# The second pair of heads turned by transposing transfers instead of by TensorE

## The chip, the cores and the metric

One core of one Trainium2 chip runs one program. Its engines are TensorE (PE: products; PEld: the loading of their stationary operand), VectorE (DVE), ScalarE (ACT), GpSimd (POOL) and SyncE (SP, here a queue that issues transfers; ScalarE issues some on a queue of its own). The metric is the time of one execution in microseconds (us). Of the kernel before there are three timed runs and one profiled execution.

## The reference, cut to what matters

Attention in which a query sees only the keys of its own cluster, then a two-layer block with a squared ReLU:

```python
B, H, S, D = 4, 8, 768, 64          # 16 clusters per head
q_assign = argmax(einsum('bhsd,hcd->bhsc', q_n, c_n))   # q_n, k_n, c_n: normalized
k_assign = argmax(einsum('bhsd,hcd->bhsc', k_n, c_n))
scores = q @ k.T / sqrt(D), and -1e9 where q_assign != k_assign
x = softmax(scores) @ v             # (B*S, H*D) = 3072 x 512
out = relu(x @ w_in) ** 2 @ w_out   # w_in 512 x 2048, w_out 2048 x 512
```

## The kernel before, in words

The attention part handles the heads in 16 pairs (four batches, four pairs each); the loop over `p` counts them from 0, and the text calls them the first, second, third and fourth pair. The second layer block follows and is not touched.

For each pair the queries and keys (128 x 768 words each) must be turned, so that the head's 64 columns lie on partitions: `qkT`, 12 blocks of 128. There are three ways in the kernel. `turn_first` turns the first pair by products with the identity, three blocks at a time, and copies them out of PSUM. `turn` (lines 289 to 303) does so for the second pair in three parts of eight products, which stand between the first pair's scores. From the third pair on, `split_words` (lines 307 to 321) lets ScalarE split each 32-bit word into its halves (two copies for the queries, two for the keys), stores them to DRAM (`words`), and `turn_words` (line 327) brings them back in one transposing transfer of 16-bit words.

A pair's steps on TensorE are then: `logits` (line 335), the products of all rows with the centroids; from them VectorE finds each row's cluster (`turn_logits`, `number`, lines 340 to 380), and the cluster numbers, called marks, go out (`far`) and come back (`rows`) by small transfers on SyncE. Nine tiles follow, counted from 0: six of 512 query columns and three that hold the last 256 twice. Each tile is a mask product of marks (line 456) and a score product (line 447) added in one PSUM bank; ScalarE takes the exponential (line 463) into `ex`, VectorE adds them up (line 466). Then come the products with V (line 481), the sums (line 500) and their reciprocals, which go to DRAM (`far_r`) and come back spread over partitions (`rb`). The banks of the scores (`ps_sc`) number three, and the logits and the sums of a pair take one of them in turn: tile n can begin when the exponential of tile n - 3 is done. The first pair's marks are not numbers but a one-hot tile `oh`, turned by TensorE (`turn_onehot`).

The order on every engine is the order of the code: the attention part is written as a schedule by hand. So an instruction that waits holds what stands behind it on its engine, and a transfer that waits holds the rest of its queue. The weights come in by `load_ahead` (line 128), one block in some pairs, three blocks at the start, all on SyncE.

A flag decides at the end whether a second, general program must run: `seen` holds the reciprocals of all sums, and `check_sums` counts those within bounds.

## Time and profile before

| | |
|---|---|
| timed runs | 863.5, 864.5, 865.63 us (median 864.5) |
| profiled execution | 863.94 us |
| its span | 862.0 us |
| PE busy | 852.3 us (99%) |
| DVE, ACT, POOL busy | 741.0 (86%), 452.3 (52%), 242.2 us (28%) |

The span runs from the first to the last instruction of the profile; the execution's own time is 1.94 us longer, and lies 0.56 us under the median of the timed runs. Times in the timeline are counted from the span's start.

### The profile page before, as it was taken

To read this page: it belongs to the slowest core of one execution; us is meant where nothing else is said; L and a number is where in the kernel's file an instruction comes from. 1 tells how busy PE (TensorE), PEld (TensorE's weight loads), DVE (VectorE), ACT (ScalarE), POOL (GpSimd) and SP (SyncE) were. 2 spreads that over 40 slices of the span, in tenths; PEclk is the share of its full clock that TensorE was granted. 3 is DMA by queue.
4 is the path that set the end of the run, shared out by engine and by line. 5 is a ranking of instruction groups with operands and counts; after the bars stand their busy time and mean duration, and the time that the engine had idled before them with its cause. 6 is when DMAs were issued, how large, how long until landed. Compare 5 with 4: busy or idle time off the path is not lost.

```text
span 862.0 us, 15526 instructions
## 1 busy us (share of the span) xinstructions
PE 852.3 (99%) x5883; PEld 648.9 (75%) x5883; DVE 741.0 (86%) x1189; ACT 452.3 (52%) x697; POOL 242.2 (28%) x202
## 2 busy tenths in 40 slices
PE   9999999999999999999999999999999999999997
PEld 5454444444444455557899999999999999999997
DVE  6798888888888899999779988789888898887786
ACT  5877766777775557752212692222269322693120
POOL 0000000000000046762466737130223902237000
PEclk9999999999999999999999999999999999999999
DMA  7787798677666217729895554459447895433542
GB/s 258 162 194 201 216 268 197 183 198 196 177 176 178 64 61 249 241 85 336 329 336 195 206 186 152 179 162 337 149 183 230 288 379 191 183 140 137 214 153 71
DMA packets 149443, 173.30 MB, mean 201 GB/s; under 512 B 57226, under 2 KB 126962, under 8 KB 146034
## 3 DMA queue, kind: packets, MB, share of 16 engines
q1 hardware_dynamic: 132802, 151.89, 55.8%
q10 hardware_dynamic: 16560, 20.35, 7.3%
q8 instruction: 48, 0.79, 0.4%
q14 instruction: 33, 0.27, 0.1%
HBM read 110.93 MB, written 50.27 MB: 187 GB/s over the span
## 4 chain that ended last, share of the span: by engine, by line
PE 88%; DVE 6%; DMA 2%; issue 1%; ACT 1%; POOL 1%; SPq 0%; DVEq 0%; POOLq 0%
PE bank L1365 23%; PE bank L1098 15%; PE sc L447 14%; PE av_a L481 10%; PE bank L1262 6%; PE av_b L481 5%; PE more L1098 5%; PE sc L456 4%; PE bank L811 3%; PE sc L335 1%; PE sc L500 1%; DMA wt<-w_far 1%; DVE g L1177 1%; DVE w_raw L155 1%; DVE g L767 1%
## 5 line engine op out<-in xcount | busy, mean ns | idle before, releaser
L463 ACT ACTIVATE ex<-sc 128x1024 f32<-128x1024 f32 x144 | 144.4, 1026 | 38.0 <-PE sc L447 31.9
L447 PE MATMUL sc<-qkT 64*128 64x512 f32 (+1 forms) x768 | 151.0, 484 | 0.0
L167 POOL TENSOR_TENSOR w_in<-w_in,w_raw 128x512 int32<-128x512 int32 x16 | 21.4, 1338 | 294.4 <-DVE w_in L159 278.2
L1083 POOL TENSOR_TENSOR g<-g,home 128x768 f32<-128x768 f32 x30 | 55.7, 1876 | 152.4 <-DVE home L1177 102.2
L447 PEld LDWEIGHTS sc<-qkT 64*128 64x128 f32 x768 | 67.1, 188 | 41.0 <-issue 29.8
L481 PE MATMUL av_a<-ex,v_raw 128*64 128x512 f32 x384 | 85.9, 596 | 0.0
L466 DVE TENSOR_TENSOR total<-total,ex 128x1024 f32<-128x1024 f32 x64 | 78.7, 1229 | 6.5
L1613 ACT COPY spare<-bank 128x128 f32<-128x128 f32 x35 | 9.2, 263 | 136.5 <-issue 84.8
L1365 PE MATMUL bank<-wt,l 128*128 128x128 f32 x544 | 72.0, 275 | 0.4 <-DVE l L557 0.4
L1365 PE MATMUL bank<-wt,home 128*128 128x128 f32 x552 | 70.5, 275 | 0.0
L1365 PEld LDWEIGHTS bank<-wt,l 128*128 128x128 f32 x544 | 66.2, 192 | 0.6 <-issue 0.5
L1365 PEld LDWEIGHTS bank<-wt,home 128*128 128x128 f32 x552 | 66.0, 192 | 0.0
L1177 DVE TENSOR_TENSOR g<-bank,g 128x384 f32<-128x384 f32 (+2 forms) x108 | 53.7, 506 | 13.0 <-PE bank L1098 8.4
L481 PEld LDWEIGHTS av_a<-ex,v_raw 128*64 128x64 f32 x384 | 26.2, 137 | 51.0 <-issue 50.3
L1067 ACT COPY home<-bank 128x384 f32<-128x384 f32 x66 | 30.9, 480 | 56.4 <-PE bank L1098 55.7
L456 PE MATMUL sc<-rows 64*128 64x512 bf16 (+1 forms) x360 | 60.5, 323 | 0.0
L787 ACT ACTIVATE g<-g 128x768 f32<-128x768 f32 (+1 forms) x77 | 55.7, 723 | 2.4
L786 ACT ACTIVATE g<-g 128x768 f32<-128x768 f32 (+1 forms) x77 | 54.8, 711 | 2.3 <-DVE g L1177 1.2
L481 PE MATMUL av_b<-ex,v_raw 128*64 128x256 f32 x384 | 44.2, 379 | 0.0
L456 PEld LDWEIGHTS <-rows 64*128 64x128 bf16 x360 | 18.5, 94 | 33.0 <-issue 29.2
L481 PEld LDWEIGHTS av_b<-ex,v_raw 128*64 128x64 f32 x384 | 27.6, 137 | 20.7 <-issue 5.7
L1365 PE MATMUL bank<-wt,g 128*128 128x128 f32 x304 | 38.8, 275 | 0.0
(296 smaller groups left out, 1852.5 us busy)
## 6 DMA issues: line engine op xcount, KB each, us to landing
wt<-right_far SPq DMA_DIRECT2D x11, 1792.0 KB
wt<-w_far SPq DMA_DIRECT2D x20, 896.0 KB
words<-flat SPq DMA_DIRECT2D x26, 384.0 KB
w_raw<-in_moe_w_in_dram SPq DMA_DIRECT2D x16, 512.0 KB
w_raw<-in_moe_w_out_dram SPq DMA_DIRECT2D x16, 512.0 KB
wt<-right_far SPq DMA_DIRECT2D x7, 1024.0 KB
v_raw<-in_v_dram SPq DMA_DIRECT2D x16, 384.0 KB
rb<-far_r SPq DMA_DIRECT2D x30, 192.0 KB
```

The lines of the kernel that those rows point to most:

```text
L447: nc.tensor.matmul(sc[i][:, e, cols], lhsT=qkT[pair][rows, NCH + c], rhs=qkT[pair][rows, n.start // P : n.stop // P], start=first, stop=no ...
L456: nc.tensor.matmul(sc[i][:, e, cols], lhsT=ohT[pair][rows, 1, c * P : (c + 1) * P], rhs=ohT[pair][rows, 0, columns(i)], start=first, stop= ...
L463: nc.scalar.activation(out=ex[i], in_=sc.pop(i), func=ACT.Exp, scale=SCALE)
L466: eng.tensor_tensor(out=out, in0=a, in1=b, op=ALU.add)
L481: nc.tensor.matmul(bank[D * e : D * (e + 1), 0 : n.stop - n.start], lhsT=raw_v[pair][:, e, c], rhs=ex[i][:, e, cols], start=c == 0, stop=c ...
L786: nc.scalar.activation(out=to, in_=to, func=ACT.Relu)
L787: nc.scalar.square(to, to)
L1083: nc.gpsimd.tensor_tensor(out=of_four(to, s)[:, :, half], in0=of_four(base, s)[:, :, half], in1=beside[s].rearrange("p u m n -> p (u m) n" ...
L1098: nc.tensor.matmul(bank[:, QT * u : QT * (u + 1)], lhsT=lefts[j, s](u)[i], rhs=operand[i], start=begins and u == 0, stop=True, skip_group_ ...
L1177: nc.vector.tensor_tensor(out=out, in0=one, in1=two, op=ALU.add)
L1262: nc.tensor.matmul(bank, lhsT=left[j][:, f], rhs=right(j)[:, f], start=begins and f == 0, stop=True, skip_group_check=True,)
L1365: nc.tensor.matmul(bank, lhsT=left[:, f], rhs=rhs[:, f], start=(f == 0), stop=(f == F4 - 1))
```

## The change

The second pair is turned like the later ones: ScalarE splits it at the very start (into two tiles of `ex` instead of `flat`), issues the two stores on its own queue, and SyncE brings it back in two transposing transfers of half the size. `turn` is gone. The first pair's one-hot marks are set directly where a logit equals the row's maximum, without choosing among equal maxima; `count_marks` counts them, and another count than one per row makes the flag call the general program. The copy of the first pair's last three blocks is shared by ScalarE and VectorE (`by_two`). In the first pair the scores of all three first tiles come ahead of the masks, and the second pair's logits stand behind the eighth tile, in the bank `M`. The second pair scores two tiles ahead of its masks. Moved on SyncE's and ScalarE's queues: the second pair's rows go ahead of the third pair's turning, as before; V of the second pair is loaded behind that; of three weight blocks one is loaded in the first pair and two in the second; the fourth pair's keys are split in the second pair, behind the third tile, and the fifth pair's loads follow there.

```diff
-    seen = const.tile([P, NG * NBL], F32, name="seen")
+    seen = const.tile([P, NG * NBL + 1], F32, name="seen")
-    def turn(pair, part, bank):
...
-                nc.tensor.matmul(
-                    bank[D * e : D * (e + 1), P * i : P * (i + 1)],
-                    lhsT=raw[pair][which][:, e, c], rhs=ident, start=True, stop=True,
-                )
-        nc.scalar.copy(
-            out=qkT[pair][:, 4 * part : 4 * part + 4].rearrange("p c n -> p (c n)"), in_=bank
-        )
...
     def split_words(pair, which, queue=nc.sync):
-        flat = loads.tile([P, NCH, 2, 2 * D], U16, name="flat", tag="qk")
+        if pair == 1:
+            spare = expp.tile([P, 2, 512], F32, name="ex").bitcast(U16)
+            flat = spare.rearrange("p a n -> p (a n)")[:, 0 : 4 * S // 2].rearrange(
+                "p (c two d) -> p c two d", c=NCH, two=2
+            )
+        else:
+            flat = loads.tile([P, NCH, 2, 2 * D], U16, name="flat", tag="qk")
...
     def turn_words(pair):
-        nc.sync.dma_start(
-            qkT[pair].rearrange("p c n -> p (c n)").bitcast(U16),
-            words.pop(pair).rearrange("c p two d -> (c p two) d"), transpose=True,
-        )
+        far = words.pop(pair)
+        for i in range(0, 2 * NCH, NCH if pair == 1 else 2 * NCH):
+            c = slice(i, i + (NCH if pair == 1 else 2 * NCH))
+            nc.sync.dma_start(
+                qkT[pair][:, c].rearrange("p c n -> p (c n)").bitcast(U16),
+                far[c].rearrange("c p two d -> (c p two) d"), transpose=True,
+            )
...
     def number(pair):
         nc.vector.reduce_max(out=mx, in_=src, axis=AX.X)
+        if pair == 0:
+            nc.vector.tensor_tensor(
+                out=oh.rearrange("p b e c -> p (b e) c")[:, :, 0:C], in0=src, in1=over_c(mx),
+                op=ALU.is_ge,
+            )
+            return
...
+    def count_marks():
+        marked = small.tile([P, 1], F32, name="marked")
+        nc.vector.reduce_sum(
+            out=marked, in_=oh.rearrange("p b e c -> p (b e) c")[:, :, 0:C], axis=AX.XY
+        )
+        nc.vector.tensor_scalar(
+            out=seen[:, NG * NBL :], in0=marked, scalar1=2.0 * NBL, scalar2=0.5,
+            op0=ALU.is_equal, op1=ALU.mult,
+        )
...
-    turn_first(1, 1, halves[1], nc.vector.tensor_copy)
+    turn_first(1, 1, halves[1], by_two)
     logits(0, begin("ls"))
-    for i in ("oh", 0, 1):
+    for i in range(2):
         begin(i)
     turn_logits(0)
     number(0)
+    for i in range(2):
+        split_words(1, i, nc.scalar)
...
         if p == 0:
+            turn_words(1)
             load_qk(3)
-            load_ahead(0)
+            load_ahead(-2)
...
-        load_v(p + 1)
         if p:
+            load_v(p + 1)
             load_ahead(p - 1)
         if p == 0:
             for i in range(2):
-                turn(1, i, (V, M)[i])
                 score(p, i, 0, True)
             turn_onehot()
+            count_marks()
             for t in rows_of:
                 nc.vector.memset(t, 0.0)
-            turn(1, 2, V)
+            begin(2)
+            score(p, 2, 0, True)
             for i in range(NB):
-                if i == 2:
-                    begin(i)
-                    score(p, i, 0, True)
                 mask(p, i, 0, False)
                 exponential(i)
+        elif p == 1:
+            for i in range(2):
+                begin(i)
+                score(p, i, 0, True)
+            for i in range(2):
+                mask(p, i, 0, False)
+                exponential(i)
+            tile_of(p, 2)
+            split_words(3, 1)
+            turn_words(3)
+            load_qk(4, (nc.scalar, nc.scalar))
...
         for i in range(NCH, NCH + NB):
             tile_of(p, i)
+            if p == 0 and i == NCH + 1:
+                sc["ls"] = M.rearrange("p (a n) -> p a n", a=1)
+                logits(1, sc["ls"])
+                turn_logits(1)
+                number(1)
+                turn_words(2)
+                load_v(1)
+                add(nc.vector, first, first, ex[NCH - 1])
...
         if p == 0:
             split_words(3, 0)
-        split_words(p + 3, 1)
-        load_qk(p + 4, (nc.scalar, nc.scalar))
+        else:
+            split_words(p + 3, 1)
+            load_qk(p + 4, (nc.scalar, nc.scalar))
```

What moves on three engines, as the two programs list their instructions. First TensorE, from the first pair's logits on, before (a score tile is two products of line 447):

```order
L335 MATMUL sc<-qkT,cnT 32x384 x4
L295 MATMUL av_a<-ident,q_raw 64x128 x8
L447 MATMUL sc<-qkT 128x512 x2
L295 MATMUL av_b<-ident,q_raw 64x128 x4
L295 MATMUL av_b<-ident,k_raw 64x128 x4
L447 MATMUL sc<-qkT 128x512 x2
```

and with the change, where the second pair's logits (`av_b` is the bank `M`) stand far behind, between the first pair's last two tiles:

```order
L328 MATMUL sc<-qkT,cnT 32x384 x4
L450 MATMUL sc<-qkT 128x512 x4
```

```order
L450 MATMUL sc<-qkT 128x256 x2
L328 MATMUL av_b<-qkT,cnT 32x384 x4
L459 LDWEIGHTS ex
L459 MATMUL sc<-ex 128x256
```

The turning products of the second pair are gone, eight more of them behind the turning of the one-hot marks too, and the scores follow the logits directly.

Second ScalarE, from the last exponentials of the first pair to the fourth one of the second pair, before:

```order
L463 ACTIVATE ex<-sc 128x1024 x3
L315 COPY flat<-q_raw 128x12x64 x2
L315 COPY flat<-k_raw 128x12x64 x2
L95 DMA q_raw<-in_q_dram 128x2x384
L95 DMA k_raw<-in_k_dram 128x2x384
L139 ACTIVATE w_in<-w_raw 128x512
L145 ACTIVATE w_raw<-w_raw 128x512
L490 COPY xT<-av_a 128x512
L490 COPY xT<-av_b 128x256
L463 ACTIVATE ex<-sc 128x1024 x6
```

and with the change:

```order
L466 ACTIVATE ex<-sc 128x1024 x3
L305 COPY flat<-q_raw 128x12x64 x2
L139 ACTIVATE w_in<-w_raw 128x512
L145 ACTIVATE w_raw<-w_raw 128x512
L493 COPY xT<-av_a 128x512
L493 COPY xT<-av_b 128x256
L466 ACTIVATE ex<-sc 128x1024 x3
L305 COPY flat<-k_raw 128x12x64 x2
L95 DMA q_raw<-in_q_dram 128x2x384
L95 DMA k_raw<-in_k_dram 128x2x384
L466 ACTIVATE ex<-sc 128x1024 x3
```

The split of the fourth pair's keys and the fifth pair's loads have moved from behind the first pair's exponentials to between the second pair's third and fourth.

Third SyncE, from the third pair's turning to the third pair's rows (`rows_167`), before:

```order
L327 DMA_TRANSPOSE qkT<-words 128x3072
L316 DMA words<-flat 128x6x256 x2
L515 DMA far_r<-seen 128x12
L327 DMA_TRANSPOSE qkT<-words 128x3072
L522 DMA rb<-far_r 64x768 x2
L105 DMA v_raw<-in_v_dram 128x2x384
L383 DMA far<-marks_t 128x3x32
L386 DMA rows_167<-far 3x4x384 x2
```

and with the change:

```order
L320 DMA_TRANSPOSE qkT<-words 128x3072
L105 DMA v_raw<-in_v_dram 128x2x384
L306 DMA words<-flat 128x6x256
L518 DMA far_r<-seen 128x12
L525 DMA rb<-far_r 64x768 x2
L105 DMA v_raw<-in_v_dram 128x2x384
L128 DMA w_raw<-in_moe_w_in_dram 128x1024 x2
L306 DMA words<-flat 128x6x256
L320 DMA_TRANSPOSE qkT<-words 128x3072
L376 DMA far<-marks_t 128x3x32
L379 DMA rows_167<-far 3x4x384 x2
```

The second store of the fourth pair and its turning now stand behind the spreading, a load of V and two weight loads, directly ahead of the third pair's marks and rows.

## Rows read from the trace of the kernel before

**Rows 1.** The page's first part: busy us (share of the span) xinstructions.

```profile
PE 852.3 (99%) x5883; PEld 648.9 (75%) x5883; DVE 741.0 (86%) x1189; ACT 452.3 (52%) x697; POOL 242.2 (28%) x202
```

**Rows 2.** Timeline of PE, first pair: start us, us, engine line op out<-in xcount.

```profile
9.32 1.09 PE L295 MATMUL av_a<-ident,q_raw 128*64 128x128 f32 x16
10.35 1.13 PE L447 MATMUL sc<-qkT 64*128 64x512 f32 x4
...
15.29 0.61 PE L456 MATMUL sc<-ex 64*128 64x512 bf16 x4
...
16.97 0.85 PE L335 MATMUL sc<-qkT,cnT 128*32 128x384 f32 x8
17.89 0.39 PE L456 MATMUL sc<-ex 64*128 64x512 bf16 x2
```

**Rows 3.** Timeline of PE, first pair's products with V to third pair's masks.

```profile
24.48 5.37 PE L481 MATMUL av_a<-ex,v_raw 128*64 128x512 f32 x24
...
33.15 0.39 PE L456 MATMUL sc<-rows 64*128 64x512 bf16 x2
...
39.54 0.38 PE L456 MATMUL sc<-rows 64*128 64x512 bf16 x2
...
53.29 0.79 PE L456 MATMUL sc<-rows 64*128 64x512 bf16 x2
```

**Rows 4.** Timeline of ACT, first pair; in brackets idle time before and what ended it.

```profile
6.87 0.48 ACT L285 COPY qkT<-sc 128x384 f32<-128x384 f32 x1 [0.18 <-PE sc L280]
...
14.04 0.87 ACT L410 ACTIVATE ex<-sc 128x384 bf16<-128x384 bf16 x2 [0.90 <-PE sc L402]
...
15.89 2.86 ACT L463 ACTIVATE ex<-sc 128x1024 f32<-128x1024 f32 x3
...
22.24 1.55 ACT L315 COPY flat<-q_raw 128x768 uint16<-128x768 uint16 x2
...
26.36 1.94 ACT L463 ACTIVATE ex<-sc 128x1024 f32<-128x1024 f32 x2 [0.46 <-ACT flat L315]
```

**Rows 5.** Timeline of DVE: the first pair's copy, the third pair's marks.

```profile
7.95 0.56 DVE L285 COPY qkT<-sc 128x384 f32<-128x384 f32 x1 [0.52 <-PE sc L280]
...
38.58 0.58 DVE L346 STREAM_TRANSPOSE lt<-sc 128x384 f32<-128x384 f32 x1 [0.77 <-PE sc L335]
...
42.50 0.28 DVE L379 STREAM_TRANSPOSE marks_t<-marks 128x96 bf16<-128x96 bf16 x1
```

**Rows 6.** Timeline of SyncE's queue: start and length of each issue.

```profile
23.24 0.38 SPq L383 DMA_DIRECT2D far<-marks_t  x1
26.61 1.68 SPq L386 DMA_DIRECT2D rows<-far  x2
28.76 6.77 SPq L327 DMA_TRANSPOSE qkT<-words  x1
...
40.01 3.70 SPq L327 DMA_TRANSPOSE qkT<-words  x1
...
50.48 1.52 SPq L386 DMA_DIRECT2D rows<-far  x2
52.05 1.00 SPq L316 DMA_DIRECT2D words<-flat  x2
...
56.32 2.75 SPq L327 DMA_TRANSPOSE qkT<-words  x1
...
64.79 1.52 SPq L386 DMA_DIRECT2D rows<-far  x2
66.42 0.38 SPq L105 DMA_DIRECT2D v_raw<-in_v_dram  x1
...
75.64 3.21 SPq L327 DMA_TRANSPOSE qkT<-words  x1
```

**Rows 7.** Stretches of time: busy us per engine, PEclk, DMA share, GB/s.

```profile
9.00:11.00 2.00, 2.00 (x22) 1.15 (x20) 1.50 (x3) 0.54 (x1) 0.00 (x0) 1.00 1.07 386
...
58.00:59.00 1.00, 1.00 (x9) 0.64 (x7) 0.97 (x5) 0.95 (x2) 0.00 (x0) 1.00 1.21 276
```

More of the change, by code (lines that the diff above doesn't have):

```diff
@@ L287, in turn_first @@
             raw.pop(0)
-    def turn(pair, part, bank):
-        if part == 0:
-            qkT[pair] = qktp.tile([P, 2 * NCH, P], F32, name="qkT")
-        for i in range(4):
-            which, c = divmod(4 * part + i, NCH)
-            for e in range(2):
-                nc.tensor.matmul(
-                    bank[D * e : D * (e + 1), P * i : P * (i + 1)],
-                    lhsT=raw[pair][which][:, e, c], rhs=ident, start=True, stop=True,
-                )
-        nc.scalar.copy(
-            out=qkT[pair][:, 4 * part : 4 * part + 4].rearrange("p c n -> p (c n)"), in_=bank
-        )
-        if part == 2:
-            raw.pop(pair)
     words = {}
@@ L362, in number @@
         nc.vector.reduce_max(out=mx, in_=best, axis=AX.X)
-        if pair == 0:
-            nc.vector.tensor_tensor(
-                out=oh.rearrange("p b e c -> p (b e) c")[:, :, 0:C], in0=best, in1=over_c(mx),
-                op=ALU.is_equal,
-            )
-            return
         squared = small.tile([P, n], F32, name="squared")
@@ L395, in turn_onehot @@
         )
-        for half, bank in enumerate((sc.pop("oh")[:, 0], M)):
+        for half, bank in enumerate((V, M)):
             n = NBL // 2
@@ L607, in load_ahead, with by_two @@
             loaded += 1
+    def by_two(out, in_):
+        nc.scalar.copy(out=out[:, 0:QT], in_=in_[:, 0:QT])
+        nc.vector.tensor_copy(out=out[:, QT:], in_=in_[:, QT:])
+    QT = TB // 2
     centroids_norm()
@@ L639 @@
                 early_x_sums()
-            turn_words(p + 2)
+            if p > 1:
+                turn_words(p + 2)
             spread(p - 1)
@@ L671 @@
             tile_of(p, NB)
-        if p < 2:
             logits(p + 1, begin("ls"))
@@ L679 @@
                 tile_of(p, i)
-            add(nc.vector, first, first, ex[i])
+            if p or i + 1 < NCH:
+                add(nc.vector, first, first, ex[i])
         if p == 0:
@@ L683 @@
                 split_words(2, i, nc.scalar)
-            turn_words(2)
         else:
@@ L1675, in check_sums @@
         nc.vector.tensor_scalar(
-            out=flag[0:1], in0=every, scalar1=UP * float(P * NG * NBL), scalar2=None, op0=ALU.is_lt
+            out=flag[0:1], in0=every, scalar1=UP * float(P * (NG * NBL + 1)), scalar2=None, op0=ALU.is_lt
         )
```

## The prediction

> **What bounds the kernel now.** I read the page's first part, then the timeline engine by engine around the change. TensorE is busy for 99% of the span [rows 1], and in its timeline each group begins before or as the one ahead of it ends; the largest gap shown is 0.07 us, at 17.82 [rows 2]. The kernel is one TensorE queue, and a microsecond counts only if it leaves or enters that queue. So for each edit I ask whether TensorE loses work, or begins to wait. The three it can wait for are ScalarE (the exponentials that free the three score banks) [rows 4], VectorE (the marks) [rows 5], and SyncE's one ordered queue of transfers [rows 6]. At the third pair's masks TensorE is already at the edge: that row lasts 0.79 us for two products, where the second pair's lasts 0.39 [rows 3], because the marks' rows are sent only at 50.48 [rows 6].
>
> **What it removes.** Eight turning products hold TensorE from 9.32 to 10.35, 1.03 us [rows 2]. Twenty-four go: 3.1 us. ScalarE loses their three copies, VectorE three short operations in the first pair and half of a copy; TensorE waited for none of them.
>
> **What it adds at the start.** ScalarE now has, in this order: half of the last copy (from 7.95 on [rows 5], at half of 0.48 us [rows 4], to 8.2), the second pair's two splits with their stores, and the two copies of the turned marks. For the third pair, splits and stores took from 22.24 to 26.36 [rows 4], 4.12 us, gaps around the issues included; the copies of the marks take 0.87. So the first pair's masks begin at 8.2 + 4.12 + 0.87 = 13.2 instead of 15.29 [rows 2]. TensorE meanwhile scores three tiles (1.1 us each [rows 2]) and turns the marks, and is through at about the same time. The first exponential begins 0.60 after the masks (15.29 to 15.89 [rows 2, 4]) and lasts about 1.0 (2.86 for three, overlapping). Its bank is what tile 3 waits for: 13.25 + 0.60 + 1.05 + 0.05 = 14.95, against 17.89. Before, the second pair's logits stood in that hole (16.97 to 17.89 [rows 2]); now it is empty, and the logits, 0.85, come later, after tile 7. Six tiles took 24.48 - 17.89 = 6.59 [rows 2, 3], so the products with V begin at 14.95 + 6.59 + 0.85 = 22.4 instead of 24.48: **2.1 of the 3.1 us** are gained, 1.0 has become waiting for ScalarE.
>
> The second pair's logits fall at 20.3 (five tiles after 14.95). Its second store is issued at about 12.2. Two stores and their landing take 52.05 to 56.32 [rows 6], 4.3; one, with 1 us less data, about 3.3: 15.5. A whole turning with all that is sent behind it takes 56.32 to 64.79, 8.5, so half of one at most 4.2: 19.7. In time, by 0.6 us at the least; cost nothing, and if late, a rival below. The counting of the marks (a reduction like the 0.56 us ones and one small operation) lies on VectorE while it waits for the first exponentials; weight loads 2 and 3 and V's second load move out of the first 20 us, which only matters where they go.
>
> **The second pair.** Logits at 20.3, VectorE 0.9 later, 4.2 us of marks (38.58 to 42.78 [rows 5]): 25.4. Marks to rows took 3.4 (23.24 to 26.61 [rows 6]) beside two stores; here 2.7, since the stores are earlier: 28.1; masks 2.8 later (50.48 to 53.29 [rows 3, 6]): 30.9. TensorE is there at 22.4 + 8.67 (24.48 to 33.15 [rows 3]) = 31.05, and scores two tiles first, 2.0: 33.05. No wait. But in this pair ScalarE splits the fourth pair's keys between the exponentials of tiles 2 and 3. Exponentials from 33.05 + 0.60; three to 36.5; the split 1.55 [rows 4] to 38.0; tile 3's exponential to 39.0. Tile 5 needs its bank (the third pair's logits take one in between): 39.0, against 39.54 before [rows 3]. TensorE alone would have come 2.1 sooner, at 37.4. So another 1.5 us becomes waiting, and **0.55 us** of gain is left.
>
> **The third pair's rows.** This is the term that decides. SyncE's order is now: rows of the second pair (28.1 to 29.8), turning for the third pair (2.75 [rows 6]: 32.6), V, the first store of the fourth pair, reciprocals (33.8; behind the store in the queue, landed by 36.5), then the reciprocals' spreading (1.2), V, two weight loads, the second store, and only after its landing the turning for the fourth pair; behind that, the marks of the third. Before, that turning began at 40.01 and the rows went at 50.48. Its price is not in the trace and needs bounds. Upper: one V load, one weight load and two stores took 66.42 to 75.64 [rows 6], 9.2, beside two loads on ScalarE's queue; a weight load is 0.13 MB larger than a store; so 36.5 + 1.2 + 9.2 + 0.35 = 47.3, and 48.5 if the reciprocals are late too. Lower: at the 386 GB/s of the first loads [rows 7], V, two weights and a store (0.39 + 1.05 + 0.39 MB) are 4.8 us; a store's fixed part is 4.3 less 2.0 of data = 2.3; so 36.5 + 1.2 + 4.8 + 2.3 = 44.8. I take 44.8, since the two loads on ScalarE's queue go out here some 2 us before the weights. From a turning to the rows behind it: 8.5 with the spreading between (56.32 to 64.79); less its 1.2, 7.3. So rows at 52.1, masks 2.8 later at 54.9, against TensorE's own 53.29 - 0.55 = 52.7: a wait of 2.2 us, and **1.6 us later than before**. Afterwards the order is the old one, and a saturated TensorE neither regains nor loses.
>
> The turning's speed is one place to weigh. With only a turning in flight the queues moved 276 GB/s (58 to 59 us), where the first loads moved 386 [rows 7]; its 0.79 MB therefore cost 2.85 us, not 2.0. The Trainium skill (Advanced Engine Details and Errata, X-Bar Transpose) says that transposing transfers are as fast as regular ones on trn2; the trace does not agree. By that rule the third pair's rows would come 0.8 us sooner and the sum would be 0.8 us slower than before instead of 1.6.
>
> Sum against the profiled execution: 863.94 - 3.1 + 1.0 + 1.5 + 2.2 = 865.5. The three runs shown have a median 0.56 above it: **866.1**.
>
> **Rivals.** (1) *The queue is slower than I took it*: the turning for the fourth pair starts near 47 (the row with mixed traffic), rows at 54.3, masks at 57.1, 3.8 later than before: 868.3. It decides from a turning later than 45.8, since then the masks come after 55.9, over 2.6 us (0.3%) late. For it: the two weight loads moved there, and every mixed stretch in [rows 6]; against: the shorter queue beside it. It ends slower. The Trainium skill (VectorE: DVE Perf Modes, Rules for kernel authors) points the same way: 128x128 turning belongs on TensorE if PSUM is a possible destination, as it was; no run here shows it yet. (2) *The queue keeps up*: rows before 50, TensorE waits at no mask, and 0.55 stays: 863.9. Against it: 7.3 us from any turning to rows, so the turning would have to start before 42.6. (3) *All 3.1 us stay*: ScalarE's waits vanish in slack I do not see: 861.4. Against it: tile 3 cannot start before an exponential that follows 4.1 us of splitting. (4) *The half turnings land late*: if each takes the 6.77 us that one issue lasted in the trace's worst case, the logits wait some 2 us, and all behind them, the queue too: 1.6 + 2 = 3.6 later, 868.1. (5) *The change does something else*: two equal maxima in the first pair would now set the flag and run the second program, far slower; with random data next to nothing.
>
> **How the numbers follow.** The forecast with its own range of 864.3 to 867.0 has a chance of 0.50; (1) 0.29, (2) 0.10, (3) 0.06, (4) 0.04, (5) 0.01. Within 0.3% of 864.5 (2.6 us, about what a measurement of this kernel can tell from no change): 0.60; slower 0.34; faster 0.06. The range of 863.0 to 869.5 takes in (2), (1) and (4) and leaves out (3) and the upper bound at 48.5.
>
> **What would show it.** Right: a hole of about 1 us on TensorE between the first pair's masks and its tile 3; tile 5 of the second pair behind an exponential that stands behind the split; the third pair's masks waiting for rows, 1 to 2 us after 53.3. Wrong: third pair's masks before 53 (then the queue was overpriced), or a wait at the second pair's logits or masks (then the half turnings or the marks were underpriced), or the fourth pair's turning issued after 46.

## The result, and the profile after

The changed kernel takes 875.89 us (median of six runs, 873.83 to 877.28), the kernel before, run beside it, 865.07 (six runs, 863.5 to 866.51). The ratio is 1.0124, 95% interval [1.0109, 1.0138]: 10.8 us slower. The forecast was 866.1, its range ended at 869.5. The profiled execution took 874.99 us with a span of 873.1, 11.1 more than before. One of e15's runs below (5084 us), one of e2's (880.83) and two of the kernel before's beside e1 to e4 (1809) were slow for a reason that is not known, and the ratios leave them out, while the medians count them.

TensorE's work fell by the 48 matmuls of the 24 products and as many weight loads (the page's first part, busy us and share of the span; before in [rows 1]):

```profile
PE 852.5 (98%) x5835; PEld 647.8 (74%) x5835; DVE 741.2 (85%) x1188; ACT 453.4 (52%) x699; POOL 242.8 (28%) x202
```

The busy time did not fall with it (852.3 us before), because other products took longer: the first ones of the kernel, at a granted clock that reads 1.00 (last section), and those behind a long wait, at a lower one. The timeline of PE shows where the time went; first three rows of before (others in [rows 2, 3]), then after:

```profile
7.83 1.56 PE L335 MATMUL sc<-qkT,cnT 128*32 128x384 f32 x8
...
43.97 5.37 PE L481 MATMUL av_a<-ex,v_raw 128*64 128x512 f32 x24
...
82.62 5.37 PE L481 MATMUL av_a<-ex,v_raw 128*64 128x512 f32 x24
```

```profile
4.49 1.55 PE L280 MATMUL av_a<-ident,q_raw 128*64 128x128 f32 x12 [0.51 <-DMA q_raw<-in_q_dram]
...
8.81 1.71 PE L328 MATMUL sc<-qkT,cnT 128*32 128x384 f32 x8
...
15.64 0.39 PE L459 MATMUL sc<-ex 64*128 64x512 bf16 x2 [0.68 <-ACT ex L466]
...
21.14 0.85 PE L328 MATMUL av_b<-qkT,cnT 128*32 128x384 f32 x8
...
23.12 5.37 PE L484 MATMUL av_a<-ex,v_raw 128*64 128x512 f32 x24
...
31.01 0.85 PE L503 MATMUL sc<-total,ups 128*32 128x384 f32 x8
...
44.00 5.37 PE L484 MATMUL av_a<-ex,v_raw 128*64 128x512 f32 x24
...
58.63 1.51 PE L328 MATMUL sc<-qkT,cnT 128*32 128x384 f32 x8 [6.67 <-DMA qkT<-words]
59.88 1.54 PE L503 MATMUL sc<-total,ups 128*32 128x384 f32 x8
61.35 0.84 PE L459 MATMUL sc<-rows 64*128 64x512 bf16 x2
...
90.74 5.37 PE L484 MATMUL av_a<-ex,v_raw 128*64 128x512 f32 x24
```

The first pair's products with V begin at 23.12 instead of 24.48, although the first logits came 0.98 us late (8.81 instead of 7.83). At 44.00 the second pair's products with V stand where they stood before (43.97), and then TensorE waits 6.67 us for the fourth pair's turned words. The logits and sums behind that wait take 1.51 and 1.54 us instead of 0.85 (21.14 and 31.01 above). The stretches of time show why (us, busy us of PE, PEld, DVE, ACT, POOL, granted clock, DMA share, GB/s):

```profile
52.00:56.00 4.00, 0.00 (x0) 0.00 (x0) 1.16 (x3) 0.69 (x2) 1.28 (x1) 0.83 1.05 161
56.00:60.00 4.00, 1.37 (x12) 0.58 (x16) 0.00 (x0) 0.00 (x0) 0.00 (x0) 0.50 0.66 139
60.00:64.00 4.00, 3.98 (x26) 1.69 (x20) 2.39 (x6) 0.92 (x1) 0.00 (x0) 0.82 0.65 199
```

While TensorE waits, the granted clock falls to 0.50, which is 1.2 GHz, and comes back within the last stretch. The turned words are late because of SyncE's queue (before in [rows 6]):

```profile
27.97 1.67 SPq L379 DMA_DIRECT2D rows<-far  x2
29.76 3.42 SPq L320 DMA_TRANSPOSE qkT<-words  x1
33.22 1.42 SPq L105 DMA_DIRECT2D v_raw<-in_v_dram  x1
...
39.26 1.17 SPq L525 DMA_DIRECT2D rb<-far_r  x2
40.52 0.53 SPq L105 DMA_DIRECT2D v_raw<-in_v_dram  x1
41.10 0.94 SPq L128 DMA_DIRECT2D w_raw<-in_moe_w_in_dram  x2
42.09 0.43 SPq L306 DMA_DIRECT2D words<-flat  x1
50.29 6.22 SPq L320 DMA_TRANSPOSE qkT<-words  x1
...
58.70 1.53 SPq L379 DMA_DIRECT2D rows<-far  x2
```

The fourth pair's second store goes out at 42.09, and the turning that needs it only at 50.29, 10.3 us later than before. A count of bytes tells why. Stretches before, then after:

```profile
10.00:14.00 4.00, 4.00 (x41) 2.14 (x38) 2.79 (x6) 1.18 (x2) 0.00 (x0) 1.00 1.05 387
...
20.00:28.00 8.00, 8.00 (x62) 4.25 (x60) 7.48 (x13) 6.91 (x9) 0.00 (x0) 1.00 0.34 95
```

```profile
10.00:14.00 4.00, 4.00 (x26) 1.66 (x24) 2.43 (x6) 3.06 (x5) 0.00 (x0) 1.00 0.44 124
...
20.00:28.00 8.00, 8.00 (x58) 3.31 (x56) 7.35 (x14) 7.10 (x10) 0.00 (x0) 1.00 0.83 259
```

Before, the fourth pair's queries and keys (0.79 MB), three weight blocks (1.57) and V (0.39) were loaded by 20 us, at 387 GB/s from 10 to 14, and the transfers then rested (95 GB/s). After, SyncE's queue stands at the second pair's half turnings until ScalarE has split, the transfers idle at 124 GB/s, and the stores and turnings of the second pair (0.79 MB each way) come first. The fourth pair's queries and keys and one weight are made up for by 28 us; V and two weights, 1.44 MB, are not. They stand ahead of the fourth pair's second store. It is the order of the queue that leaves them there: from 28 to 32 us the transfers rest once more, while SyncE's queue is at the marks' rows and the third pair's turning (27.97 to 33.18):

```profile
28.00:32.00 4.00, 4.00 (x38) 1.98 (x36) 2.50 (x4) 2.40 (x5) 0.00 (x0) 1.00 0.27 50
```

The rest of the loss is far behind, in the second block, whose code is the same. The timeline of PE there, before and after:

```profile
596.71 1.47 PE L1098 MATMUL bank<-xT,w_in 128*128 128x192 f32 x8
...
604.51 1.46 PE L1098 MATMUL bank<-wt,w_in 128*128 128x192 f32 x8
```

```profile
604.62 1.47 PE L1127 MATMUL bank<-xT,w_in 128*128 128x192 f32 x8
607.52 0.89 PE L1127 MATMUL bank<-wt,raw 128*128 128x192 f32 x4 [1.43 <-DVE x_t L560]
609.44 0.89 PE L1127 MATMUL bank<-wt,home 128*128 128x192 f32 x4 [1.03 <-DVE spare L560]
...
615.37 1.46 PE L1127 MATMUL bank<-wt,w_in 128*128 128x192 f32 x8
```

From the first of these rows to the last it takes 7.80 us before and 10.75 after. So the 11.1 us are 0.98 at the start, 7.14 from the first logits to the fourth pair's products with V (82.62 - 7.83 before, 90.74 - 8.81 after), 2.95 here, and next to nothing in the rest. The first 0.98 is not the change: copies of the kernel before start as late (the table's first logits).

### The profile page after: what moved, and what is told of

Its sections match the earlier page's. It is cut to its first block, busy times and chain, and to the rows that moved or that the text cites. A ratio compares the mean times of both kernels' runs of the same rounds, so it can differ in the third digit from the quotient of the medians.

```text
span 873.1 us, 15432 instructions
## 1 busy us (share of the span) xinstructions
PE 852.5 (98%) x5835; PEld 647.8 (74%) x5835; DVE 741.2 (85%) x1188; ACT 453.4 (52%) x699; POOL 242.8 (28%) x202
## 3 DMA queue, kind: packets, MB, share of 16 engines
q10 hardware_dynamic: 18128, 21.14, 7.3%
## 4 chain that ended last, share of the span: by engine, by line
PE 82%; DVE 8%; DMA 4%; issue 2%; ACT 2%; POOL 1%; SPq 0%; DVEq 0%; ACTq 0%; POOLq 0%
PE bank L1394 22%; PE bank L1127 16%; PE sc L450 14%; PE av_a L484 9%; PE more L1127 5%; PE av_b L484 4%; PE bank L1291 4%; PE sc L459 4%; PE bank L840 2%; PE sc L328 1%; PE sc L503 1%; DMA qkT<-words 1%; DMA words<-flat 1%; DVE spare L1206 1%; DMA w_raw<-in_moe_w_out_dram 1%
```

## The experiments

The table has, for each kernel, its median, its ratio to the kernel before run on the same chip (95% interval), and from its profile: when the first logits began; the attention part from there to the fourth pair's products with V, against 74.79 us before; and the second block's stretch, 7.80 us before.

| kernel | us | ratio | first logits | attention | stretch |
|---|---|---|---|---|---|
| changed kernel | 875.89 | 1.0124 [1.0109, 1.0138] | 8.81 | +7.14 | 10.75 |
| e1_weights_first | 874.01 | 1.0092 [1.0068, 1.0115] | 9.95 | +6.32 | 12.57 |
| e2_split_first | 874.12 | 1.0087 [1.0059, 1.0114] | 8.98 | +4.69 | 12.12 |
| e3_both | 870.38 | 1.0063 [1.0043, 1.0083] | 8.00 | +1.69 | 10.03 |
| e4_loads_later | 876.87 | 1.0114 [1.0082, 1.0147] | 10.41 | +7.27 | 12.00 |
| e5_before_four_more | 866.22 | 1.0011 [0.9997, 1.0025] | 9.78 | -0.46 | 7.80 |
| e6_both_four_more | 870.38 | 1.0055 [1.0038, 1.0072] | 10.64 | +2.19 | 9.74 |
| e7_weights_at_start | 870.0 | 1.0045 [1.0028, 1.0062] | 10.63 | +3.46 | 12.34 |
| e8_start_four_more | 869.1 | 1.0041 [1.0023, 1.0058] | 10.52 | -0.19 | 12.74 |
| e9_before_moved | 866.24 | 0.9997 [0.9981, 1.0012] | 9.59 | -0.51 | 7.80 |
| e10_after_unmoved | 875.98 | 1.0109 [1.0081, 1.0136] | 9.75 | +9.84 | 12.17 |
| e11_start_unmoved | 868.42 | 1.0032 [1.0011, 1.0053] | 8.47 | +2.05 | 12.25 |
| e12_loads_behind | 872.4 | 1.0075 [1.0049, 1.0101] | 7.97 | +1.93 | 10.81 |
| e13_before_dram | 864.99 | 0.9993 [0.9979, 1.0006] | 10.39 | -0.50 | 7.80 |
| e14_after_dram | 873.96 | 1.0091 [1.0066, 1.0116] | 10.91 | +8.15 | 7.80 |
| e15_order | 869.5 | 1.0034 [1.0016, 1.0052] | 9.98 | -1.63 | 10.22 |
| e16_order_dram | 866.6 | 1.0013 [0.9998, 1.0029] | 10.82 | -1.05 | 10.65 |
| e17_order_nops | 866.08 | 1.0004 [0.9992, 1.0015] | 9.78 | +0.64 | 7.80 |
| e18_before_nops | 866.89 | 1.0021 [1.0006, 1.0036] | 10.49 | -0.48 | 8.57 |

### What delays the fourth pair's turning

**e1_weights_first** loads all three blocks in the first pair.

```diff
-            load_ahead(-2)
+            load_ahead(0)
```

> All three weight blocks are loaded in the first pair again, none of them ahead of the fourth pair's second store. Theory A (the two blocks, 1.05 MB, delay that store, and the turning that waits for it): the store lands some 4 us sooner (1.05 MB at 276 to 386 GB/s is 2.7 to 3.8 us), the turning is issued near 46.5 instead of 50.29, TensorE's wait at the fourth pair's logits falls from 6.67 to about 2.9 us, its clock falls for less time, and the time is 870 to 872 us. Theory B (ScalarE splits the fourth pair's keys too late; the store is issued at 42.09 whatever stands ahead): the turning not before 48.5, the wait over 5 us, the time 874 to 876 us.

**e2_split_first** puts the fourth pair's second split, its turning and the fifth pair's loads back where they were.

```diff
-            if p > 1:
-                turn_words(p + 2)
+            turn_words(p + 2)
...
             tile_of(p, 2)
-            split_words(3, 1)
-            turn_words(3)
-            load_qk(4, (nc.scalar, nc.scalar))
...
-        else:
-            split_words(p + 3, 1)
-            load_qk(p + 4, (nc.scalar, nc.scalar))
+        split_words(p + 3, 1)
+        load_qk(p + 4, (nc.scalar, nc.scalar))
```

> The fourth pair's keys are split in the first pair again, their store and the turning stand behind the second pair's reciprocals as in the kernel before; the two weight blocks stay in the second pair, now behind the turning. Theory B (the late split is the cause): the turning is issued near 40, no wait at the fourth pair's logits, no fall of the clock, and the gain of the start is kept as far as the third pair's rows allow: 861 to 865 us. Theory A (the weight blocks are the cause): they now delay only the rows of the third pair's marks behind them; rows at 52 to 53 instead of 50.48 before, the third pair's masks wait 2 us, and the time is 865 to 868 us. In either case the second block's extra 2.9 us go with the wait, if they follow from the shift.

**e3_both** has both edits.

> Both edits together. If A and B each are a part of the delay, this is the fastest of the four: the turning for the fourth pair at 40 or before, rows of the third pair by 50.5, no wait at logits or masks over 1 us, and what the start gains (about 2 us at the first pair's products with V) is kept in part: 862 to 864 us. If the start is the loss (the half turnings or the splits beside the three weight loads), the second pair's logits wait and the time is 865 us or more.

**e4_loads_later** moves only the sixth pair's loads.

```diff
-            load_qk(p + 4, (nc.scalar, nc.scalar))
+            if p > 1:
+                load_qk(p + 4, (nc.scalar, nc.scalar))
...
         evict(p, NCH, M)
+        if p == 1:
+            load_qk(5, (nc.scalar, nc.scalar))
```

> The sixth pair's two loads on ScalarE's queue, which were issued at 49.19 and 50.24 beside the fourth pair's turning, go behind the second pair's products with V; nothing else moves. Theory C (a turning that shares the engines with two loads takes 8.2 us to its landing, alone 5.1): it lands some 3 us sooner, at 55.5, the wait at the logits falls from 6.67 to about 3.6 us, and the time is 872 to 873 us. Without it (the turning takes its time whatever is beside it): the wait stays at 6.5, the time at 875 to 876 us.

Neither edit alone brings much, both together bring 5.5 us of the 7.14 in these profiles. Timeline of PE in e1, the third and the fourth pair's logits:

```profile
41.05 1.51 PE L328 MATMUL sc<-qkT,cnT 128*32 128x384 f32 x8 [3.13 <-DMA qkT<-words]
...
59.03 0.85 PE L328 MATMUL sc<-qkT,cnT 128*32 128x384 f32 x8 [0.95 <-DMA qkT<-words]
```

In e1 the wait has moved one pair forward: the weights now stand ahead of the second pair's rows and the third pair's turning. Theory A had foreseen the 0.95 as 2.9, and the 3.13 not at all. Nor did the fourth pair's turning go out near 46.5: with no weights ahead of its store it was issued at 50.79, and the wait behind it is short because TensorE itself came late. In e2, SyncE's queue and the third pair's masks:

```profile
46.96 0.93 SPq L128 DMA_DIRECT2D w_raw<-in_moe_w_in_dram  x2
47.93 0.43 SPq L376 DMA_DIRECT2D far<-marks_t  x1
54.81 1.53 SPq L379 DMA_DIRECT2D rows<-far  x2
```

```profile
57.14 0.39 PE L459 MATMUL sc<-rows 64*128 64x512 bf16 x1 [3.76 <-DMA rows<-far]
```

The turning is in time there, and the weights hold the third pair's marks instead: marks to rows takes 6.9 us. So there is no single culprit. The bytes that were not moved by 20 us delay whatever stands behind them. Even in e3 the second pair's masks wait 2.2 us for their rows. e4 leaves open what the loads beside the turning cost: the wait fell from 6.67 to 6.02, not to 3.6, and the turning landed 7.2 us behind its issue instead of 8.2, but the loads went out only 1.5 us behind it, so they still shared the engines with it.

If it is bytes and their order, the cure is to fill the idle stretch at 10 to 14 us and to put last what is needed last.

**e7_weights_at_start**, **e11_start_unmoved** and **e12_loads_behind** issue the weights ahead of the half turnings (e11 and e12 also have an edit of the next section, which did nothing; e12 moves the fifth pair's loads too).

```diff
-            turn_words(1)
-            load_qk(3)
-            load_ahead(0)
+            load_ahead(0)
+            turn_words(1)
+            load_qk(3)
```

> Both edits, with the three weight loads ahead of the second pair's turning on SyncE's queue, where they can run while the queue waits for ScalarE's splits. Theory H (with the half turnings at the head of the queue the engines of the transfers stand idle for some 3 us at 10 to 13 us, 15 to 83 GB/s, and what they did not move there comes later, ahead of the third pair's rows): the second pair's rows are issued near 27 instead of 30.25, the fourth pair's turning near 40 instead of 43.5, the third pair's masks wait under 0.5 us instead of 2.2, and the time is 867 to 869 us. Rival S (the weights now delay the second pair's stores and turnings): the second pair's logits wait 1 us or more, and the time is 870 us or more.

> Both edits and the weights ahead of the half turnings, with the on-chip addresses of the kernel before. Theory P: the second block costs nothing more than before; what is left is the attention part, which stood at -0.2 and +3.5 us in the two looks at this order: 865 to 868 us. Rival D: 869 to 870.5 us.

> As the kernel before this one, and the fifth pair's two loads on ScalarE's queue go behind the first pair's products with V instead of ahead of them, so that nothing stands beside the store of the second pair's marks, which took 3.0 and 4.6 us to land. If that store is what holds the rows and the third pair's turning: it lands in 2 us, the turning for the fourth pair is issued some 1.5 us sooner, no wait at the third pair's masks, and the time is 863 to 866 us. If the loads only collide with the third pair's turning instead: no gain over its neighbour.

The attention part came out at +3.46, -0.19 (e8, the same order), +2.05 and +1.93: no better than e3 on the whole. By the ratios (1.0032 to 1.0045 for e7, e8 and e11, 1.0063 and 1.0055 for e3 and e6, with overlapping intervals) a small gain is possible. In e11 and e12 the second pair's logits waited 0.8 to 1.1 us for the half turnings, so three blocks are too many to put ahead (rival S in part). e12's own edit gained nothing; its median is 4 us above e11's.

**e15_order** puts one block ahead of the half turnings, one behind the fourth pair's rows, and the third, with V, behind the third pair's marks.

```diff
+            load_ahead(-2)
             turn_words(1)
             load_qk(3)
-            load_ahead(0)
+            load_ahead(-1)
...
-        if p:
+        if p > 1:
             load_v(p + 1)
             load_ahead(p - 1)
...
             number(p + 1)
+            load_v(p + 1)
+            load_ahead(p - 1)
```

> Both edits, one weight block ahead of the half turnings and one behind the fourth pair's loads, and in the second pair V's load and the last of the three blocks behind the third pair's rows instead of ahead of them. Theory H (what stands ahead of the rows on the transfers decides): the third pair's rows are issued near 50, no wait over 0.5 us at the second pair's logits and the third pair's masks, and the attention part ends 1 us sooner to 0.5 us later than before; with the second block's waits as in all copies of the changed kernel (2 to 5 us), 867 to 869 us. If H is wrong: the third pair's masks wait 2 us as with both edits alone, 870 us.

SyncE's queue in e15:

```profile
50.01 1.52 SPq L379 DMA_DIRECT2D rows<-far  x2
```

The rows go at 50.01, as expected, TensorE waits 1.05 us at the third pair's logits and at no mask, and the attention part is 1.63 us shorter than before. The same order gave -1.05 and +0.64 in two later profiles (e16, e17): a gain that the spread between executions nearly covers. So the order of the transfers, with the place of the fourth pair's split, made the loss of 7.14 us; with both mended, the turning by transfers neither clearly gains nor clearly loses.

### What delays the second block

In every copy of the changed kernel up to e16, but for e14, the stretch is 2 to 5 us longer; in no copy of the kernel before, until e18, is it. SyncE's waits there name the transfer (engine, line, what it waited for: us in total, times, longest). Before, then after:

```profile
SPq L1740 <- DMA out_dram<-g: 0.2, 1, 0.2
```

```profile
SPq L1769 <- DMA out_dram<-g: 8.8, 2, 6.9
```

After, the load of x (L1769) waits 6.9 us until a store of ScalarE's queue has landed; behind it stand the loads of raw and home, for which TensorE waits. (Its rows above name VectorE's sums, which came last by a hair; raw landed at 607.38 and home at 609.30, just ahead of their products at 607.52 and 609.44.) Load and store share no data. In the trace the transfers of both queues signal on eight semaphores in turn, and each waits until the last user of its own has landed: the load goes out at 600.42, and the store that had its semaphore last, issued at 590.29, lands at 600.36. The change adds four transfers and shifts that round by half.

**e5_before_four_more** adds four transfers to the kernel before; **e6_both_four_more** and **e8_start_four_more** add them to e3 and e7, which closes the round of eight again.

```diff
+        if 9 <= p < 13:
+            nc.sync.dma_start(extra[p - 9 : p - 8], odd[0:1])
```

> The kernel before, with nothing but four transfers of 8 bytes added on SyncE late in the attention part (one in each of four pairs), which nobody reads: as many as the change adds. Theory L (each transfer takes the next of eight completion semaphores in turn and waits until the transfer that had it last has landed; four more shift every later one by half a round, and a load of x in the second block then stands behind a store of ScalarE's queue): the same waits for raw and home as in the changed kernel appear at the second block's end at some 598 us, and the kernel becomes 2 to 5 us slower, 867.5 to 870. Rival R (those waits follow from the later start of everything, or from chance): no waits there, 864 to 866.5 us.

> The kernel with both edits (all three weight blocks and the fourth pair's split in the first pair), and the same four transfers of 8 bytes, so that the second block's transfers have the semaphores again that they had before the change. Theory L: the waits for raw and home at 608 us go, and the time falls from 870.4 by 2 to 4 us, to 866 to 868. Rival R: the waits stay, 870 to 871.

> All of it: both edits, the weights ahead of the half turnings, and the four transfers of 8 bytes. If L and H both hold, what the start gains (2 us) is kept and nothing is lost behind it: 862.5 to 865 us, at or under the kernel before. If only L holds: 866 to 868; if only H: 867 to 869.

Theory L fell on both sides: 7.80 in e5, 9.74 and 12.74 in e6 and e8. Next the addresses: the wider seen moves every later tile on the chip by 32 bytes, and the second pair's words move every later tile in DRAM by 0.79 MB.

**e9_before_moved** and **e10_after_unmoved**:

```diff
-    seen = const.tile([P, NG * NBL], F32, name="seen")
+    seen = const.tile([P, NG * NBL + 8], F32, name="seen")[:, 0 : NG * NBL]
```

```diff
-        ss = const.tile([P, 1], F32, name="cen_ss")
+        both = const.tile([P, 2], F32, name="cen_ss")
+        ss = both[:, 0:1]
...
-        rden = const.tile([P, 1], F32, name="cen_rden")
+        rden = both[:, 1:2]
```

> The kernel before, with the tile seen allocated eight columns wider and those columns not used: every tile of on-chip memory behind it (xT, x_t, the raw blocks of the second block, w_out, g) lies 32 bytes further on, as in the changed kernel, where the one added column of seen does it; no instruction is changed. Theory P (the place: loads into these tiles take another time, and the second block's order of transfers changes with it; the loads of xT took 7.0 us in the kernel before and in its copy with four more transfers, 5.4 to 5.5 in the changed kernels): xT's loads at 576 us land after 5.4 us instead of 7.0, TensorE waits for raw and home at 598 us, and the time is 867.5 to 870 us. Rival D (it is the place in DRAM, or the late start): no such wait, 864.5 to 866 us.

> The changed kernel, with two of its small constant tiles put into one, so that the tiles behind them have the on-chip addresses of the kernel before; the place of the tiles in DRAM stays that of the change. Theory P: no waits for raw and home at 608 us, xT's loads take 7.0 us, and the time falls by 2 to 4 us, to 872 to 873.5. Rival D: the waits stay and the time is 875 to 876.5 us.

**e13_before_dram**, and **e14_after_dram** and **e16_order_dram** (there the second pair's words get 2 ** 10 blocks):

```diff
-            words[pair] = dram.tile([2 * NCH, P, 2, 2 * D], U16, name="words")
+            words[pair] = dram.tile(
+                [4 * NCH if pair == 2 else 2 * NCH, P, 2, 2 * D], U16, ...
+            )[0 : 2 * NCH]
```

> The kernel before, whose first words tile in DRAM is given twice its size and used in its first half only: every tile of DRAM behind it lies 0.79 MB further on, at exactly the addresses of the changed kernel, where the second pair's words stand ahead of them; no instruction is changed. Theory D (the place in DRAM sets how fast transfers run there: xT's loads at 576 us took 7.0 us in the kernel before and in every copy of it, 5.4 to 5.6 in every copy of the changed kernel, and with them the order of the second block's transfers changes): xT's loads take 5.5 us, TensorE waits for raw and home at 598 us, 2 to 5 us in all, and the time is 867.5 to 870 us. Rival T (it is the changed kernel's timing, not its addresses): 7.0 us, no wait, 865 to 866.5 us.

> The changed kernel, with the second pair's words given 64 MiB of DRAM, so that every tile behind them lies exactly 64 MiB further on than in the kernel before. Theory D, if addresses count only by their lower bits: xT's loads take 7.0 us again, the waits for raw and home at 608 us go, and the time falls by 2 to 4 us, to 872 to 874. Theory D with higher bits that count too, or rival T: the waits stay, 875 to 876.5 us.

> The same order, with the tiles in DRAM 64 MiB further on than in the kernel before. If H and D (by lower bits) both hold: no wait in either part, 864 to 865.5 us, at or just under the kernel before. If D fails: as its neighbour, 867 to 869 us.

Both fell in the kernel before: 7.80 and no change of the time in e9 and e13. e10 kept the wait. e14 lost it, but e16, with the same shift in DRAM, did not, so the addresses do not decide; why e14 escaped is left open (its load of x waited 2.8 us instead of 6.9).

What is left is TensorE's program: 48 matmuls and 48 weight loads fewer and one wait more, 95 instructions. The profile counts 48 transfers of one instruction queue, 0.79 MB, 16 KB each; 11,766 matmuls and weight loads over 48 are some 250 instructions for each. The Trainium skill (Advanced Engine Details and Errata, ISA Cache) gives 16 KB as 256 instructions, and the trace comes near it. The profile counts these fetches on the same 16 engines as the data. The transfers of the kernel before while x is loaded (queue, kind: packets, MB, share of 16 engines; from 576.4 to 583.4):

```profile
q1 hardware_dynamic: 426, 1.82, 78.7%
q10 hardware_dynamic: 740, 0.36, 17.4%
q8 instruction: 1, 0.02, 0.8%
```

In the changed kernel the list for the same loads, 584.3 to 589.8, has no instruction row: the first load of x lands after 5.4 us there instead of 7.0, and what follows goes out 1.8 us sooner, beside ScalarE's stores instead of behind them. All profiles agree. In the kernel before and its copies e5, e9 and e13 such a fetch begins 4.1 us behind the issue of x, and the next load goes out 7.8 to 7.9 us behind it; in the changed kernel and its copies up to e16 the fetch begins at 6.7, and the next load goes out at 6.0 to 6.4. ScalarE's next stores begin 5.56 us behind the issue of x in both, so they do not make the difference.

**e17_order_nops** is e15 with 95 idle instructions on TensorE's queue, **e18_before_nops** the kernel before with 161 (256 - 95).

```diff
+        if p in range(2, 7):
+            for _ in range(19):
+                nc.tensor.nop(hint="pad", nofuse=True)
         for i in range(NCH):
             times_v(p, i, V)
```

> The kernel of e15_order with 95 instructions that do nothing on TensorE's queue (19 ahead of the products with V of five early pairs): the change had made TensorE's program 95 instructions shorter, and this gives it its old length ahead of the second block. Theory F (TensorE's program is fetched by transfers of 16 KB, one for some 256 instructions, on the same engines as the data; the shorter program moves the fetches against the loads: in the kernel before one falls at 580.5 us into the loads of xT, in every copy of the changed kernel none does, xT is 1.5 us sooner there, the loads behind it fall on ScalarE's stores, and raw and home come late): fetches at the places of the kernel before, xT's loads take 7.0 us again, no waits for raw and home, and the time falls from 869.5 to 864 to 866 us. Rival T (the second block's waits follow from something else that the change does): xT's loads 5.5 us, the waits stay, 869 to 870 us.

> The kernel before with 161 instructions that do nothing on TensorE's queue (23 ahead of the products with V of seven early pairs): 256 less 95, so that the fetches fall where they fall in the changed kernel. Theory F: xT's loads take 5.5 us instead of 7.0, TensorE waits for raw and home at 598 us, 2 to 5 us in all, and the time is 867.5 to 870 us. Rival T: xT's loads 7.0 us, no wait, 865 to 866.5 us.

SyncE's waits at the load of x in e17, and in e18:

```profile
SPq L1770 <- DMA out_dram<-g: 0.2, 1, 0.2
```

```profile
SPq L1743 <- DMA out_dram<-g: 5.7, 2, 3.9
```

Timeline of PE in e18, the kernel before with idle instructions:

```profile
601.68 0.89 PE L1101 MATMUL bank<-wt,home 128*128 128x192 f32 x4 [0.45 <-DMA home<-raw_far]
```

For the waits, theory F holds in both directions. Ninety-five instructions that do nothing bring the fetch from 6.7 to 4.1 us behind the issue of x and the stretch from 10.22 to 7.80; 161 of them bring it from 4.1 to 6.5, and the kernel before gets the waits for a store and for home. By themselves the idle instructions cost nothing: from the first logits to the stretch, e18 takes 588.5 us, e5, e9 and e13 588.7 to 589.0. What the fetch is worth in time is less sure. The ratio goes from 1.0034 to 1.0004 with the idle instructions, but e16, which has none and keeps its wait (10.65), stands at 1.0013, within noise of both; and the size was too large: e18's stretch grew by 0.77 us and its median by 1.5, not 2 to 5. That the fetch acts through the loads of x and ScalarE's stores is read from these rows, not tested by itself.

No version beats the kernel before: e17 is the changed kernel with order and fetches mended, and ties with it, within [0.9992, 1.0015].

## Why the prediction was wrong

1. *3.1 us removed*: right, the products are gone.
2. *The start*: right. Less the 0.98 us by which the first logits came late here, tile 3 stands at 14.66 (14.95 forecast) behind a hole of 0.68 (1.0), the second pair's logits at 20.16 (20.3) without a wait, the products with V at 22.14 (22.4).
3. *The second pair*: right in its sum, less so in its parts. The rows were in time, and at its products with V 0.95 us of gain was left (43.97 before, 44.00 - 0.98 after); forecast 0.55. The wait for an exponential behind the split came at tile 6 and took 0.74 us, not 1.5 at tile 5; a wait of 0.42 for the third pair's turned words, ahead of its logits, had no term.
4. *The third pair's rows*, called the term that decides: **this step failed, in its size**. I took the lower bound, a turning at 44.8. It was issued at 50.29, less the late start 49.3, beyond both upper bounds. Of the 4.5 us, 1.8 came from the reciprocals, which I had landed by 36.5 and whose spreading went at 39.26; 2.7 came from V, two weights and the store, priced at 7.1 us and taking 9.8 (40.52 to 50.29). The reason I gave for the lower bound, that ScalarE's two loads go out some 2 us ahead of the weights, came true for the second one (39.13, the weights at 41.10) and did not help. From 40 to 50 us the transfers moved 2.63 MB, that load's 0.39 among them, at 263 GB/s with the engines 90% busy; I had priced 1.83 MB at the 386 GB/s of the first loads. The timeline of ACT, the stretch, and its list by queue (SyncE's transfers are on q1, ScalarE's on q10):

```profile
36.67 0.39 ACTq L95 DMA_DIRECT2D q_raw<-in_q_dram  x1
...
39.13 0.39 ACTq L95 DMA_DIRECT2D k_raw<-in_k_dram  x1
```

```profile
40.00:50.00 10.00, 9.37 (x68) 4.82 (x69) 9.41 (x14) 8.07 (x10) 0.00 (x0) 1.00 0.90 263
```

```profile
q1 hardware_dynamic: 1504, 2.23, 76.1%
q10 hardware_dynamic: 272, 0.39, 13.9%
```

   The Trainium skill (DMA: Bandwidth & Descriptors, Queues, rings and completion order) says that SyncE's and ScalarE's queues run on the same 16 engines, and these rows agree.

   I also looked for the wait at the marks. It fell 2.7 us ahead of them, on the turned words, which I had not timed: 8.3 us from the turning's issue to the logits. The wait was 6.67 instead of 2.2, and the fall of the clock, not in the sum at all, added about 1.3 (the rows last 0.66 longer at the logits and 0.69 at the sums). With 0.4 more gain ahead, that is some 5.5 of the 9.5 us by which the profiled execution missed the sum of 865.5.
5. *The turning's speed* mattered less than what stood beside it: the fourth pair's took 8.2 us from issue to landing here, beside two loads, the one at 56.32 before 5.1. The rule of equal speed would have moved the sum by 0.8 us; the queue moved it by 4.5.

Rival 1 (a slower queue, decided by a turning later than 45.8) was what happened, but its wait came at the turned words and not at the marks, and my bound of 48.5 for it was too low. The sign named for it, a turning issued after 46, came true. I had priced each transfer at the queue's head; I had not counted what the engines would not have moved by 20 us, though [rows 7] show them full there before. The other 4 us had no term: 2.95 in the second block, and 0.98 at the start, which is spread between executions and not the change.

## What to carry to other kernels

Where transfers run near their limit, count bytes by stretch before timing a queue: a transfer that waits at a queue's head leaves the engines idle, and the missing bytes come out later, ahead of whatever stands behind them; loads that depend on nothing belong ahead of it, but no more of them than fit in the gap. A wait of several us on TensorE can cost more than itself: here the granted clock fell to 0.50 in one of 6.67 us, and that added about 1.3. A loss far from an edit, in unchanged code, can come from the program's length alone: padding the engine's queue with idle instructions is a cheap test for it.

## What the runs showed of the hardware

- The fetches of TensorE's program, 16 KB for some 250 instructions, share the engines with the data. Moving one of them by some 2.5 us took a stretch of unchanged code from 10.22 to 7.80 us (e17), and the other way from 7.80 to 8.57 (e18); with a fetch beside it, a load of x landed after 7.0 us instead of 5.4.
- A faster transfer made the kernel slower: loads that followed 1.8 us sooner met a store, and a later load that had to wait for that store's semaphore lost 6.9 us.
- The start varies by 3 us in both kernels: the first logits began between 7.83 and 10.91 us in the twenty profiles. Where they are late, the first turning products run at about half speed (1.55 us for the twelve at 4.49 here; 0.84 for twelve at 6.00 in the kernel before), while the granted clock reads 1.00 (the changed kernel):

```profile
5.00:6.00 1.00, 1.00 (x12) 1.00 (x10) 0.83 (x6) 0.78 (x2) 0.00 (x0) 1.00 1.07 386
```

  What sets this is open; it is not the change, since copies of the kernel before show it too.
